# Attention followed by two gated MLPs on one core: layer 2's weights decoded from layer 1's last eight steps on, output copies issued before their sums, weight reloads and decode buffers moved

## The chip, the cores and the metric

The kernel runs on one core of one Trainium2 chip. The metric is the device time of one execution in microseconds (us), the median of several runs. The engines are PE (TensorE, the matrix engine), DVE (VectorE), ACT (ScalarE), POOL (GpSimd) and SP (SyncE, which here only issues DMAs). Each engine works through its own queue in order; semaphores tie the queues together.

## The reference

```
attention: q, k, v are (4, 12, 448, 64); rmsnorm of q and k with g_q, g_k; softmax(q k^T / 8) v
x  = attention output as 1792 tokens x 768
x  = ((x @ w_a) * (x @ w_b)) @ w_out                      # layer 1, d_ff = 1536
out = (sigmoid(x @ w_gate) * (x @ w_val)) @ w_out2        # layer 2, same sizes
```

All six weight matrices arrive as 64-bit floats; attention's inputs are 32-bit.

## The kernel before, in words

Attention comes first and is not touched. Each layer is then done as a seven-product block scheme (2 x 2 quadrants with sums and differences of quadrants, so that seven products take the place of eight). Every product is taken in three matmuls: each operand is split into a high part (`xh`, `wh`, `gh`, made by ACT's cast) and a rest (`xl`, `wl`, `gl`, made by a subtraction on DVE), and PE adds high*high, low*high and high*low.

**First part of a layer** (`first_part`): 84 events. An event is a pair (m, p): block m of 12 (even m: w_a or w_gate, odd m: w_b or w_val), product p of 7. It has 18 matmuls (two halves of the columns, three 128-row chunks, three matmuls each), line 872. The list `events` is the order by hand. Products 1 and 2 of one m share a PSUM bank: product 2 adds onto product 1, but only after ACT has copied product 1 out (line 924, `u<-mm`). Products 6, 7 and 4 share a bank in the same way; there ACT first puts a seed into it (`mm<-u`, line 846). Product 6's copy is line 928.

**Weights of the first part** (`weights`): quadrants of the 64-bit weights are loaded into `raw` (two buffers), then decoded to 32-bit in a tile `d` by one ACT operation (line 658) and three DVE operations (659, 661, 665). Event p may need a difference of quadrants (DVE, line 720), then ACT casts `wh` (line 724) and DVE makes `wl` (line 607, the helper's line). For m of 2 and 3 two quadrants are decoded early, stored to DRAM (`bd`, line 701) and loaded again when needed (line 716). Between the events the output weights are decoded too, always into tile `d8`, and stored to DRAM (`wd`). `prepare` advances decoding and splitting by small steps between the matmuls; `decodes` may run about three events ahead.

**Left operands** (`operands`): sums of the input's quadrants (DVE, line 788, called S1 to S4), each cast (`xh`, ACT, 779) and its rest (`xl`, DVE). In layer 1 the four quadrants are loaded from DRAM by `stage_in`.

**Second part** (`second_part`): 42 steps, seven products by six blocks f. In layer 1 a step has three units of six matmuls (line 1109), in layer 2 seven tiles of three (line 1119). `step(k)` prepares the operands of step k+3: DVE difference `d` (1005), in some products a difference `u` (1023), ACT casts `wh` (1008) and `gh` (1035), DVE rests. At the last f of a product each unit's PSUM is copied out by ACT (`ah<-mm`, lines 1138, 1142, 1146); after products 6 and 7 DVE adds a sum (line 1084, `more`), and `finish` makes layer 2's input of it: an ACT cast (line 610, `xh`) and a subtraction on POOL (`xl`). The next product adds onto the same banks, so PE waits for the copies. In layer 1's last three steps `prepare(1, ..., 8)` begins layer 2's weights.

Every engine's queue is written in program order (`manual_schedule`); nothing reorders it.

## Time and profile before

| | |
|---|---|
| median of 3 runs | 1340.98 us (1340.57 to 1344.35) |
| the profiled execution | 1341.52 us, its span 1339.4 us |
| PE busy | 1250.6 us (93%) |
| DVE busy | 1004.9 us (75%) |
| ACT busy | 704.2 us (53%) |
| POOL busy | 203.6 us (15%) |
| mean granted TensorE clock | 0.977 |

The span runs from the first to the last instruction. A busy share is an average over stages: attention fills the first 320 us or so, layer 1 lies between 317 and 842 us, layer 2 after that.

### The profile page before, as it was taken

The page shows a single profiled execution, that of the slowest core. Times are in us where ns is not written, and L with a number is a line of the kernel's source. Part 1 is how long each engine was busy: PE and PEld are TensorE (multiplying, and loading weights), DVE is VectorE, ACT ScalarE, POOL GpSimd, SP SyncE. Part 2 cuts the span into 40 slices and gives each one's busy share as a digit, 9 for nine tenths or more (in the row PEclk, how much of TensorE's full clock was granted, in tenths as well). Part 3 has the DMA queues.
Part 4 walks back from the last instruction along what each step waited for, and adds up shares of the span by engine and source line. Part 5 has one row for each costly group of instructions (what it writes and reads, how often), then busy time and mean ns, then how long its engine had stood idle before and what let it go on. Part 6 is the DMA issues. An engine that isn't in the chain of part 4 may idle for free.

```text
span 1339.4 us, 19161 instructions
## 1 busy us (share of the span) xinstructions
PE 1250.6 (93%) x6468; PEld 1114.6 (83%) x6468; DVE 1004.9 (75%) x1723; ACT 704.2 (53%) x1411; POOL 203.6 (15%) x272
## 2 busy tenths in 40 slices
PE   5999998898888999999999988789999999999997
PEld 4988887787767888887888877678888888899997
DVE  7999999987686778777558686786678777567583
ACT  3888888786353343443444644543354453444643
POOL 5565567740000000000002011000000000000000
PEclk9999999999889999999999988889999999999999
DMA  5677767665613456555486552413456555486674
GB/s 139 171 178 184 186 179 199 193 154 177 234 38 121 139 167 200 172 158 182 154 285 218 167 182 70 130 59 105 128 170 200 169 171 187 142 292 219 198 251 117
DMA packets 160433, 227.20 MB, mean 170 GB/s; under 512 B 26920, under 2 KB 134992, under 8 KB 160336
## 3 DMA queue, kind: packets, MB, share of 16 engines
q1 hardware_dynamic: 160336, 225.99, 55.5%
q8 instruction: 51, 0.84, 0.3%
q14 instruction: 46, 0.38, 0.1%
HBM read 147.46 MB, written 54.35 MB: 151 GB/s over the span
## 4 chain that ended last, share of the span: by engine, by line
PE 48%; DVE 22%; DMA 10%; ACT 10%; issue 4%; POOL 2%; SPq 2%; ACTq 0%; DVEq 0%; POOLq 0%
PE mm L872 23%; PE mm L1119 10%; PE mm L1109 7%; PE pv L407 3%; PE s L332 2%; DMA wd<-d 2%; DVE d L665 2%; DVE u L896 2%; DVE wl L607 2%; DVE raw L661 2%; DMA d<-bd 2%; DVE xl L607 2%; ACT wh L724 2%; DMA qk<-in_k_dram 1%; DVE d L720 1%
## 5 line engine op out<-in xcount | busy, mean ns | idle before, releaser
L872 PE MATMUL mm<-xh,wh 128*128 128x512 f32 (+1 forms) x1008 | 376.3, 373 | 37.5 <-ACT u L924 17.1
L872 PE MATMUL mm<-xl,wh 128*128 128x512 f32 (+1 forms) x1008 | 375.0, 372 | 5.9 <-DVE xl L607 5.9
L872 PE MATMUL mm<-xh,wl 128*128 128x512 f32 (+1 forms) x1008 | 375.4, 372 | 0.3 <-DVE wl L607 0.3
L607 DVE TENSOR_TENSOR wl<-d,wh 128x384 fp32r<-128x384 f32 x252 | 144.3, 573 | 153.4 <-ACT wh L724 91.9
L872 PEld LDWEIGHTS mm<-xh,wh 128*128 128x128 f32 x1008 | 193.5, 192 | 67.5 <-ACT u L924 18.6
L872 PEld LDWEIGHTS mm<-xl,wh 128*128 128x128 f32 x1008 | 193.7, 192 | 31.2 <-DVE xl L607 7.8
L872 PEld LDWEIGHTS mm<-xh,wl 128*128 128x128 f32 x1008 | 193.3, 192 | 22.7 <-DVE wl L607 0.8
L724 ACT CAST wh<-d 128x384 fp32r<-128x384 f32 x168 | 85.9, 512 | 205.4 <-DVE d L720 196.6
L658 ACT ACTIVATE d<-raw 128x384 f32<-128x384 f32 x144 | 80.4, 558 | 98.1 <-DMA wd<-d 41.1
L1008 ACT CAST wh<-d 128x384 fp32r<-128x384 f32 x84 | 43.2, 514 | 146.0 <-PE mm L1119 43.0
L344 ACT ACTIVATE P<-s,nm 128x448 f32<-128x448 f32 x168 | 107.9, 646 | 13.3 <-DVE nm L337 12.7
L395 DVE TENSOR_TENSOR pl<-tr,ph 128x512 fp32r<-128x512 f32 (+2 forms) x168 | 100.7, 611 | 9.4 <-ACT ph L391 7.9
L337 DVE TENSOR_REDUCE nm<-s 128x1 f32<-128x448 f32 x168 | 100.1, 616 | 5.1 <-PE s L332 5.1
L1109 PE MATMUL mm<-gh,wh 128*128 128x512 f32 x252 | 95.1, 377 | 8.5 <-ACT ah L1142 4.1
L1119 PE MATMUL mm<-wh,gh 128*128 128x384 f32 x294 | 98.8, 336 | 1.0 <-ACT ah L1142 0.8
L1119 PE MATMUL mm<-wl,gh 128*128 128x384 f32 x294 | 98.6, 335 | 0.0
L1119 PE MATMUL mm<-wh,gl 128*128 128x384 f32 x294 | 98.5, 335 | 0.0
L665 DVE SCALAR_TENSOR_TENSOR d<-d,raw 128x384 uint32<-128x384 uint32 x144 | 80.2, 557 | 23.4 <-ACT d L658 13.3
L391 ACT CAST ph<-tr 128x512 fp32r<-128x512 f32 (+2 forms) x168 | 85.6, 541 | 18.3 <-PE tr L377 12.6
L1109 PE MATMUL mm<-gl,wh 128*128 128x512 f32 x252 | 94.9, 377 | 0.0
L1109 PE MATMUL mm<-gh,wl 128*128 128x512 f32 x252 | 94.5, 375 | 0.0
L661 DVE SCALAR_TENSOR_TENSOR raw<-raw 128x384 uint32<-128x384 uint32 x144 | 80.4, 559 | 3.9
(161 smaller groups left out, 2293.5 us busy)
## 6 DMA issues: line engine op xcount, KB each, us to landing
gd<-u SPq DMA_DIRECT2D x60, 448.0 KB
u<-gd SPq DMA_DIRECT2D x60, 448.0 KB
d<-wd SPq DMA_DIRECT2D x132, 192.0 KB
raw<-in_moe_w_out_dram SPq DMA_DIRECT2D x48, 384.0 KB
wd<-d SPq DMA_DIRECT2D x72, 192.0 KB
KK<-KH SPq DMA_DIRECT2D x92, 112.0 KB
raw<-in_moe_w_a_dram SPq DMA_DIRECT2D x24, 384.0 KB
raw<-in_moe_w_b_dram SPq DMA_DIRECT2D x24, 384.0 KB
```

Source lines behind the costliest of these rows:

```text
L337: nc.vector.tensor_reduce(out=d["nm"][:, t:t + 1], in_=d["ps"][t], axis=AX.X, op=ALU.max, negate=True)
L344: nc.scalar.activation(out=e, in_=d["ps"].pop(t), func=AF.Exp, bias=d["nm"][:, t:t + 1], accum_out=d["sum"][:, t:t + 1])
L391: nc.scalar.copy(out=d["x", j, z][1], in_=tr)
L395: nc.vector.tensor_tensor(out=pl, in0=tr, in1=f32(ph), op=ALU.subtract)
L607: eng.tensor_tensor(out=lo, in0=t, in1=f32(hi), op=ALU.subtract)
L658: nc.scalar.activation(out=f32(t), in_=f32(high), func=AF.Copy, scale=2.0 ** -112)
L661: nc.vector.scalar_tensor_tensor(out=low, in0=high, scalar=0x80000000, in1=low, op0=ALU.bitwise_and, op1=ALU.bitwise_or)
L665: nc.vector.scalar_tensor_tensor(out=t, in0=t, scalar=3, in1=low, op0=ALU.logical_shift_left, op1=ALU.bitwise_or)
L724: nc.scalar.copy(out=hi, in_=t)
L872: nc.tensor.matmul(ps[:, o:o + size], w[:, P * c:P * c + P], x[:, o:o + size], start=(p in (1, 5) and c == 0 and z == 0), stop=(c == KC - ...
L1109: nc.tensor.matmul(ps[:, o:o + size], w[:, P * un:P * un + P], g[:, o:o + size], start=(p in (1, 5) and f == 0 and z == 0), stop=(f == HF ...
L1119: nc.tensor.matmul(ps[:, o:o + HB], g[:, P * t:P * t + P], w, start=(p in (1, 5) and f == 0 and z == 0), stop=(f == HF - 1 and z == 2), sk ...
```

## The change

1. **Layer 2's weights begin earlier.** In `second_part` of layer 1 one small step of `prepare(1, ...)` runs in every tick of the last eight steps (six ticks in a step), in place of eight steps at once after each of the last ones. The first eight of them only let the raw loads fly. The last six steps leave tiles d0, d2, d4 to layer 2, and its decoding waits for a tile until layer 1 has given it up.
2. **Order of the first three events in layer 2**: (0,1), (1,1), (0,2) in place of (0,1), (0,2), (1,1).
3. **Output copies of all units first, then the sums**: after products 6 and 7 of a second part, ACT's copies follow each other; the sums (`more`) and `finish` go to a list of which each tick takes one.
4. **Up to four raw loads at first**: among the first ten quadrants of a layer up to four are under way, two of them in `u` tiles.
5. **Reloads moved**: the quadrants of m = 2 and 3 stored in DRAM are loaded back as soon as their tile is free (after product 7, or one event after product 4, of m - 2). Product 4's difference of quadrants is taken at product 7.
6. **Decode tiles**: output weights alternate between d5 and d8; quadrant 1 of later blocks goes to d1.
7. **A12 of layer 1** is loaded from DRAM inside the operands' first loop instead of ahead of it.

No instruction is added or taken away; each engine has the same number of them.

```
-    events = [(0, 1), (0, 2), (1, 1), (2, 1), (1, 2), (3, 1), (2, 2), (3, 2)]
+    begun = [(2, 1), (1, 2), (3, 1), (2, 2), (3, 2)]
+    orders = [[(0, 1), (0, 2), (1, 1)] + begun + events, [(0, 1), (1, 1), (0, 2)] + begun + events]
...
+        def fill():
+            while wanted and len(loaded) < (4 if total - len(wanted) < 10 and len(free_u) >= 3 else 2):
+                load()
...
+            if [t for t, _ in loaded].count(None) >= 2:
+                tag, u = take_u()
+                r = u[:, 0:2 * HB].bitcast(U32).rearrange("p (f w) -> p f w", w=2)
+            else:
+                r = rawp.tile([P, HB, 2], U32, tag="raw", name="raw")
...
-            load()
-            load()
+            fill()
+            for _ in range(1 if l == 0 else 8):
+                yield
...
-                    t = dec("d8")
+                    k += 1
+                    t = dec("d5" if k % 2 else "d8")
...
+                        if q == 1 and m >= EARLY:
+                            tag = "d1"
+                        if l == 1:
+                            while held[0] is not None and tag not in held[0]:
+                                yield
...
-                if 2 <= m < EARLY and p in (5, 4):
-                    q = 0 if p == 5 else 2
-                    B[m, q] = dec(f"d{4 * (m % 2) + q}")
-                    nc.sync.dma_start(out=B[m, q], in_=bd[l][m % 2][q // 2])
+                if again:
+                    reload(*again.pop(0))
...
+                    if p == 7:
+                        nc.vector.tensor_tensor(out=B[m, 2], in0=B[m, 2], in1=B[m, 0], op=ALU.subtract)
+                        if m + 2 < EARLY:
+                            reload(m + 2, 0)
+                        yield True
+                if p == 4 and m + 2 < EARLY:
+                    again.append((m + 2, 2))
...
+        kept_d = ("d0", "d2", "d4") if l == 0 else ()
...
+        def tick(k):
+            step(k)
+            if after:
+                after.pop(0)()
+            if l == 0 and k >= NS - 8:
+                prepare(1, max(-1, AHEAD - NS + k), 1)
...
                         nc.scalar.copy(out=sums("a", un), in_=ps)
-                        more("c", un)
-                        finish(l, 0, 1, un, unit, sums("c", un))
+                        after.append(partial(more, "c", un))
+                        finals.append(partial(finish, l, 0, 1, un, unit, sums("c", un)))
...
+                after += finals
+                finals.clear()
...
-                if l == 0 and k > NS - 4:
-                    prepare(1, AHEAD - NS + k, 8)
```

ACT's queue where product 7 of layer 1's second part ends (`ah<-mm` are the copies of the three units, `xh<-al` the casts of `finish`, `wh` and `gh` step operands, `d<-raw` a decode). Before:

```order
L1142 COPY ah<-mm 128x896
L610 CAST xh<-al 128x896
L1142 COPY ah<-mm 128x896
L610 CAST xh<-al 128x896
L1142 COPY ah<-mm 128x896
L610 CAST xh<-al 128x896
L1008 CAST wh<-d 128x384
L1035 CAST gh<-u_9226 128x896
```

The same place now:

```order
L1201 COPY ah<-mm 128x896
L673 ACTIVATE d_9340<-raw 128x384
L1201 COPY ah<-mm 128x896 x2
L1058 CAST wh<-d 128x384
L1085 CAST gh<-u_9234 128x896
L673 ACTIVATE d_9370<-raw 128x384
L613 CAST xh<-al 128x896 x3
```

The casts that wait for DVE's sums have moved behind the copies, and a decode of layer 2 has come in between the first copy and the other two.

ACT's queue from the end of layer 1's second part into layer 2's first events (`u<-mm` of line 924 is the copy of a product 1). Before:

```order
L658 ACTIVATE d_9526<-raw 128x384
L1146 COPY ah<-mm 128x896 x3
L658 ACTIVATE d_9554<-raw 128x384
L724 CAST wh<-d_9489 128x384
L658 ACTIVATE d_9566<-raw 128x384
L924 COPY u_9594<-mm 128x896
L724 CAST wh<-d_9514 128x384
L779 CAST xh<-al 128x896
L931 ACT_TABLE_LOAD
L931 ACTIVATE u_9623<-mm 128x896
```

The same place now:

```order
L763 CAST wh<-d_9403 128x384
L1205 COPY ah<-mm 128x896 x3
L673 ACTIVATE d_9568<-u_9442 128x384
L763 CAST wh<-d_9431 128x384
L968 COPY u_9594<-mm 128x896
L763 CAST wh<-d_9477 128x384
L820 CAST xh<-al 128x896
L968 COPY u_9624<-mm 128x896
L763 CAST wh<-d_9507 128x384
L673 ACTIVATE d_9639<-raw 128x384
```

One decode stands between the output copies and the first `u<-mm` where two stood, and a second copy of a product 1 has come ahead of the gate's activation.

SP's queue in layer 1, where the stored quadrants are loaded back (`d<-bd`; `gd<-u` stores gated blocks). Before:

```order
L899 DMA gd_0_1_99<-u_5594 128x896
L647 DMA raw<-in_moe_w_b_dram 128x3x256 x2
L716 DMA d_5856<-bd_0_0_230 128x384
L649 DMA raw<-in_moe_w_out_dram 128x768
L899 DMA gd_1_0_104<-u_5710 128x896
L899 DMA gd_3_0_116<-u_5674 128x896
L716 DMA d_5947<-bd_1_0_232 128x384
```

The same place now:

```order
L943 DMA gd_0_1_99<-u_5594 128x896
L739 DMA d_5651<-bd_0_0_230 128x384
L662 DMA raw<-in_moe_w_b_dram 128x3x256
L739 DMA d_5800<-bd_1_0_232 128x384
L662 DMA raw<-in_moe_w_b_dram 128x3x256
L739 DMA d_5861<-bd_0_1_231 128x384
L664 DMA raw<-in_moe_w_out_dram 128x768
```

Three reloads now stand ahead of the first output-weight load, where one reload stood ahead of it.

## Rows read from the trace of the kernel before

**Rows 1.** The page: busy shares, granted clock by fortieths of the span (tenths).

```profile
PE 1250.6 (93%) x6468; PEld 1114.6 (83%) x6468; DVE 1004.9 (75%) x1723; ACT 704.2 (53%) x1411; POOL 203.6 (15%) x272
...
PEclk9999999999889999999999988889999999999999
```

**Rows 2.** Windows, a steady stretch: busy (instructions) per engine, clock, DMA share, GB/s.

```profile
480.00:560.00 80.00, 80.00 (x394) 71.19 (x393) 64.04 (x119) 34.69 (x60) 0.00 (x0) 1.00 0.57 173
```

**Rows 3.** Windows cut at event and step borders where PE lost time.

```profile
346.83:395.11 48.28, 35.96 (x128) 29.32 (x128) 39.49 (x54) 25.01 (x35) 0.00 (x0) 0.79 0.28 93
409.74:431.08 21.34, 16.97 (x74) 13.89 (x73) 16.12 (x25) 7.40 (x13) 0.00 (x0) 0.92 0.34 115
618.76:638.28 19.52, 16.73 (x73) 14.15 (x73) 12.86 (x25) 9.02 (x16) 0.00 (x0) 0.91 0.57 185
782.62:796.26 13.64, 10.20 (x37) 8.38 (x37) 10.02 (x8) 5.79 (x7) 6.58 (x3) 0.75 0.18 60
807.27:826.78 19.51, 15.44 (x56) 12.53 (x55) 13.41 (x12) 8.84 (x13) 6.27 (x3) 0.74 0.21 68
841.46:857.39 15.93, 9.12 (x37) 7.63 (x37) 10.24 (x18) 8.88 (x13) 0.00 (x0) 0.79 0.55 167
872.02:883.95 11.93, 9.14 (x37) 7.70 (x37) 11.35 (x15) 5.94 (x9) 0.00 (x0) 0.86 0.21 73
925.66:935.70 10.04, 7.60 (x38) 6.51 (x38) 6.25 (x12) 5.28 (x9) 0.00 (x0) 1.00 0.35 114
943.03:952.48 9.45, 7.56 (x37) 6.50 (x37) 6.58 (x12) 3.81 (x7) 0.00 (x0) 1.00 0.19 47
970.80:979.90 9.10, 7.60 (x37) 6.50 (x37) 7.22 (x11) 3.25 (x6) 0.00 (x0) 1.00 0.54 178
1126.80:1144.28 17.48, 15.19 (x73) 13.00 (x73) 11.30 (x22) 8.17 (x15) 0.00 (x0) 1.00 0.54 174
```

**Rows 4.** ACT's timeline at layer 2's start: start, us, instruction, idle before.

```profile
837.11 0.58 ACT L658 ACTIVATE d<-raw 128x384 f32<-128x384 f32 x1 [2.28 <-issue]
...
850.68 0.56 ACT L658 ACTIVATE d<-raw 128x384 f32<-128x384 f32 x1 [1.30 <-DMA raw<-in_moe_w_val_dram]
851.14 0.90 ACT L924 COPY u<-mm 128x896 f32<-128x896 f32 x1
```

**Rows 5.** SP's timeline, raw loads of layer 2.

```profile
807.12 0.96 SPq L647 DMA_DIRECT2D raw<-in_moe_w_gate_dram  x2
833.80 0.37 SPq L647 DMA_DIRECT2D raw<-in_moe_w_val_dram  x1
```

**Rows 6.** Waits at the start of layer 1 (300 to 440 us), DVE and ACT.

```profile
DVE d L720 <- DMA d<-bd: 8.6, 3, 3.9
DVE raw L659 <- DMA raw<-in_moe_w_a_dram: 6.2, 3, 5.5
...
ACT d L658 <- DMA raw<-in_moe_w_a_dram: 10.0, 1, 10.0
```

**Rows 7.** DVE's waits for reloads at the start of layer 2 (840 to 980 us).

```profile
DVE d L720 <- DMA d<-bd: 11.1, 4, 3.9
```

**Rows 8.** ACT's waits for the output weights' tile, 440 to 640 us.

```profile
ACT d L658 <- DMA wd<-d: 22.4, 13, 3.9
```

**Rows 9.** Groups by line: DVE's differences of quadrants, busy us and mean ns.

```profile
L720 DVE TENSOR_TENSOR d<-d,d 128x384 f32<-128x384 f32 x96 | 53.0, 552 | 22.5 <-DMA d<-bd 22.5
```

**Rows 10.** ACT's timeline where product 7 ends in layer 1.

```profile
811.16 0.90 ACT L1142 COPY ah<-mm 128x896 f32<-128x896 f32 x1
813.41 0.94 ACT L610 CAST xh<-al 128x896 fp32r<-128x896 f32 x1 [1.36 <-DVE al L1084]
814.26 0.90 ACT L1142 COPY ah<-mm 128x896 f32<-128x896 f32 x1
```

**Rows 11.** DVE's timeline in layer 1's product 7.

```profile
781.92 1.08 DVE L1084 TENSOR_TENSOR ah<-ah 128x896 f32<-128x896 f32 x1
784.81 2.29 DVE L1084 TENSOR_TENSOR ah<-ah 128x896 f32<-128x896 f32 x1 [1.81 <-ACT ah L1138]
...
798.53 1.09 DVE L607 TENSOR_TENSOR gl<-u,gh 128x896 fp32r<-128x896 f32 x1 [0.54 <-ACT gh L1035]
...
802.10 1.09 DVE L607 TENSOR_TENSOR gl<-u,gh 128x896 fp32r<-128x896 f32 x1 [0.54 <-ACT gh L1035]
```

**Rows 12.** POOL and DVE after product 2, where three splits follow each other.

```profile
715.05 7.05 POOL L607 TENSOR_TENSOR xl<-al,xh 128x896 fp32r<-128x896 f32 x3 [404.04 <-DMA wd<-d]
...
718.92 1.20 DVE L607 TENSOR_TENSOR wl<-d,wh 128x384 fp32r<-128x384 f32 x1 [3.29 <-ACT wh L1008]
720.05 3.01 DVE L607 TENSOR_TENSOR gl<-u,gh 128x896 fp32r<-128x896 f32 x1
```

More of the change, by code (lines that the diff above doesn't have):

```diff
@@ L1 @@
 from contextlib import ExitStack
+from functools import partial
 from itertools import chain
@@ L573, in attention_then_two_gated_mlps @@
     events.append((NF - 1, 4))
-    NE = len(events)
+    orders = [[(0, 1), (0, 2), (1, 1)] + begun + events, [(0, 1), (1, 1), (0, 2)] + begun + events]
+    NE = len(orders[0])
     NS = len(PASSES) * HF
@@ L630, in weights @@
         plan = []
+        events = orders[l]
         k = 0
@@ L641, in weights @@
         loaded = []
+        total = len(wanted)
+        def fill():
+            while wanted and len(loaded) < (4 if total - len(wanted) < 10 and len(free_u) >= 3 else 2):
+                load()
         def load():
             n, j, q = wanted.pop(0)
-            r = rawp.tile([P, HB, 2], U32, tag="raw", name="raw")
+            tag = None
+            if [t for t, _ in loaded].count(None) >= 2:
[3 more added lines that the diff above has]
+                r = rawp.tile([P, HB, 2], U32, tag="raw", name="raw")
             if n < 2:
@@ L649, in load @@
                 nc.sync.dma_start(out=r.rearrange("p f w -> p (f w)"), in_=quadrant(l, n, j, q))
-            loaded.append(r)
+            loaded.append((tag, r))
         def decode(t):
-            r = loaded.pop(0)
+            tag, r = loaded.pop(0)
             t = t.bitcast(U32)
@@ L667, in decode @@
             )
-            if wanted:
-                load()
+            if tag:
+                free_u.append(tag)
+            fill()
             yield
@@ L680, in decodes @@
         def decodes():
-            e = -1
-            load()
-            load()
+            e = k = -1
+            fill()
+            for _ in range(1 if l == 0 else 8):
+                yield
             for x, m, p in plan:
@@ L694, in decodes @@
                         spilled = 2 <= m < EARLY and p < 3
-                        t = dec(f"d{4 * (m % 2) + (q + 1 if spilled else q)}")
+                        tag = f"d{4 * (m % 2) + (q + 1 if spilled else q)}"
+                        if q == 1 and m >= EARLY:
[3 more added lines that the diff above has]
+                                yield
+                            if held[0] is not None:
+                                held[0].remove(tag)
+                        t = dec(tag)
                         B[m, q] = t
@@ L707, in decodes, with reload @@
             decoded[l] = NE
+        again = []
+        def reload(m, q):
+            B[m, q] = dec(f"d{4 * (m % 2) + q}")
+            nc.sync.dma_start(out=B[m, q], in_=bd[l][m % 2][q // 2])
         def splits():
@@ L764, in operands @@
         at = where[l]
-        a, b, c12, d = (staged[l][n] for n in ("A21", "A22", "A12", "A11"))
+        a, b, d = (staged[l][n] for n in ("A21", "A22", "A11"))
         casts, rests = [], []
@@ L795, in operands @@
             to("S1", c, t[c])
+            if l == 0:
+                stage_in(0, "A12", c)
             yield
@@ L812, in operands @@
             tt(t3, d[c], a[c], ALU.subtract)
-            tt(t4, c12[c], t[c], ALU.subtract)
+            tt(t4, staged[l]["A12"][c], t[c], ALU.subtract)
             to("S4", c, t4, tag4)
@@ L836, in first_part @@
         st, late, held = {}, [], {}
+        events = orders[l]
         more = None
@@ L988, in loads @@
                 gl[k] = tag, u
-                while len(free_d) < len(W_AT[p]):
+                mine = lambda: [t for t in free_d if k < NS - HF or t not in kept_d]
+                while len(mine()) < len(W_AT[p]):
                     yield
@@ L992, in loads @@
                 for q in W_AT[p]:
-                    tag = free_d.pop(0)
+                    tag = mine()[0]
+                    free_d.remove(tag)
                     t = decp.tile([P, HB], F32, tag=tag, name="d")
@@ L1113, in second_part @@
                                 )
-                            step(k)
+                            tick(k)
                     else:
@@ L1123, in second_part @@
                                 )
-                            step(k)
+                            tick(k)
                     if f < HF - 1:
@@ L1138, in second_part @@
                         nc.scalar.copy(out=sums("a", un), in_=ps)
-                        more("c", un)
-                        finish(l, 0, 1, un, unit, sums("c", un))
+                        after.append(partial(more, "c", un))
+                        finals.append(partial(finish, l, 0, 1, un, unit, sums("c", un)))
                     elif p == 7:
                         nc.scalar.copy(out=sums("a", un), in_=ps)
-                        more("b", un)
-                        finish(l, 1, 1, un, unit, sums("b", un))
+                        after.append(partial(more, "b", un))
+                        finals.append(partial(finish, l, 1, 1, un, unit, sums("b", un)))
                     else:
@@ L1151, in second_part @@
                         seed(len(seeds))
+                after += finals
+                finals.clear()
                 del GI[k], WI[k]
                 k += 1
-                if l == 0 and k > NS - 4:
-                    prepare(1, AHEAD - NS + k, 8)
                 yield
+        assert not after
+        held[0] = None
         if l == 0:
@@ L1199, in attention_then_two_gated_mlps @@
         begin_mm("mm1", 3)
-        for n in ("A22", "A12"):
-            for c in range(KC):
-                stage_in(0, n, c)
+        for c in range(KC):
+            stage_in(0, "A22", c)
         ready[0] = True
```

9 lines of the change are left out of this document (7 added, 2 removed).

## The prediction

> **What bounds the kernel now.** I read the page first: PE is busy 93% of the span, DVE 75%, ACT 53%, and the granted clock dips in two places only, slices 11 and 12 and slices 24 to 27 [rows 1]. Those are the beginning of layer 1 and the passage from layer 1 to layer 2. What can be won must therefore be PE's idle time and slow clock there, not work: the change adds and removes no instruction. Next I took PE's pace in a steady stretch: 394 matmuls in 80 us [rows 2], so an event or a step of 18 matmuls takes 3.66 us. Then I followed the list of events and steps along PE's instructions and cut windows exactly at their borders wherever one lasted longer than that [rows 3]; a row may count a matmul or two that hang over its edge, the program has 18 to an event. The loss of a window is its length less 3.66 us for each event:
>
> - events 5 to 11 of layer 1, (3,1) to (0,7): 48.3 for 7, loss 22.7
> - events 16 to 19 of layer 1: 21.3 for 4, loss 6.7
> - events 71 to 74 of layer 1: 19.5 for 4, loss 4.9
> - layer 1's second part, first two steps of product 7: 13.6 for 2, loss 6.3
> - its last step of product 7 and the first two of product 4: 19.5 for 3, loss 8.5
> - events 0 and 1 of layer 2: 15.9 for 2, loss 8.6
> - its events 6 and 7: 11.9 for 2, loss 4.6
> - its events 18 and 19, 22 and 23, 29 and 30: 2.7, 2.1 and 1.8
> - its events 71 to 74: 17.5 for 4, loss 2.9
>
> In the windows with the largest losses the clock stands at 0.74 to 0.79, so part of each loss is matmuls at the lower level (1.2 GHz) after PE had idled; it goes when the idling goes. The waits of ACT and DVE in the same stretches then say what PE waited for.
>
> **The change part by part.**
>
> *Layer 2's start.* ACT's decode at 850.68 had waited for its raw load, and the copy of product 1 at 851.14 came right behind it in ACT's queue [rows 4]; PE's event (0,2) cannot add onto that bank before. After the change the quadrants are loaded eight steps before the end, four at a time, and event (1,1) on another bank comes between (0,1) and (0,2), so the copy has 3.66 us. The load is not the risk: one issued at 833.80 [rows 5] had its decode running at 837.11 [rows 4], 3.3 us. Its window's loss goes: -8.6. Bounds: -4, half of it, if a decode still waits ahead of the copy, and -8.6, all there is. I take the whole, since two independent edits remove the same wait.
>
> *Reloads.* DVE waited 8.6 us in three waits for reloaded quadrants in layer 1's start [rows 6] and 11.1 us in four in layer 2's [rows 7]; behind each wait stood the gates' multiplications and ACT's seeds. They now are issued at least four events (14.6 us) before their use, and the longest wait was 3.9. The losses of events 16 to 19 in layer 1 and 18 to 30 in layer 2 sum to 13.3. I take -12, since the gates behind them are a chain of DVE and ACT of their own; bounds -6 (that chain holds half) and -13.3.
>
> *Output weights' tile.* Decoding into d8 had to wait until the tile was stored: 22.4 us in thirteen waits between 440 and 640 us, the longest 3.9 [rows 8]. Most lie under PE's work; where two output tiles follow each other, in events 71 to 74, they reach PE. With two tiles in turn a store has a whole decode more. The two windows lose 4.9 and 2.9: I take -7, bounds -3 (the raw load, still two deep there, is late next) and -7.8. Tile d1 now serves quadrant 1 of odd blocks too; its last reader is three events older, so I cost that at nothing, covered by those 11 us.
>
> *Four raw loads at the start of layer 1.* ACT waited 10.0 us in one piece for a raw load, DVE 5.5 [rows 6], while the input's quadrants were being loaded ahead of it. The ninth and tenth weight quadrants are now issued before those. But the loss of events 9 to 11 is DVE's: it makes the sums and rests of the operands one after the other, and PE takes them as they come. What PE gains is what DVE stands idle less, 5.5, less the two product-4 differences that now come earlier in DVE's queue at 0.55 each [rows 9]: -4.4. Bounds: 0 (another load is late instead) and -10.0. Moving A12's loads behind the others lies under the same DVE work and costs nothing; without that cover it would cost the three loads' time, which the upper bound holds.
>
> *Copies before sums.* Before, each unit's copy waited for the unit before it: copy 811.16, DVE's sum, cast 813.41, next copy 814.26 [rows 10]. Now the three copies follow each other, 0.90 each, and a unit of PE is 1.22, so after product 6 PE should not wait: -6.3. But the work only moves. DVE has three sums of 1.08 to do, and POOL's three splits then come back to back and hold DVE up: the second sum took 2.29 [rows 11], and in the 7.05 us of three splits after product 2 DVE got one operation done and a second begun [rows 12]. So DVE falls about 3 + 5 = 8 us behind. It cannot recover: in product 7 its step takes 802.10 - 798.53 = 3.57 [rows 11] against PE's 3.66. At the end of product 7 ACT's first copy stands behind the operands for three steps later, which wait for DVE, and is late by what DVE is: I let the second window keep its 8.5 and take -6.3 + 0.3 = -6. Bounds: 0 (both windows keep theirs, in other places) and -14.8 (both go).
>
> The Trainium skill speaks against this part ("SBUF — State Buffer", Who interferes with whom): a DVE operation with two SBUF inputs and a POOL operation that reads SBUF exclude each other for a whole instruction. The rows agree with it for a subtraction. By the rule the two-input operations of layer 2's decoding, which now stand among product 4's splits, are shut out as well, and the sum would be that of rival 1; by the rows alone, which show no such operation beside POOL, it is the one below.
>
> *Not changed:* events 6 to 11 of layer 2. DVE's order of sums there is the old one and begins at the same distance behind PE: 0, between -4.6 and +4. Layer 2's second part: 0, within 1.
>
> **The sum.** 8.6 + 12 + 7 + 4.4 + 6 = 38.0. The profiled execution took 1341.5 (span 1339.4 and 2.1 around it), so 1303.5; the median shown is 0.5 lower: 1303. By the favourable bounds the gain is 8.6 + 13.3 + 7.8 + 10 + 14.8 + 4.6 = 59, by the others 4 + 6 + 3 + 0 + 0 - 4 = 9.
>
> **Rivals.**
> 1. *DVE is the next bound and gives back what the moves win.* The windows with DVE nearly always busy (11.35 of 11.93 us in events 6 and 7 of layer 2 [rows 3]) speak for it. Then layer 1's passage gains 0, layer 2's start 4 (its decodes end late), layer 1's start 0: 38 - 6 - 4.6 - 4.4 = 23, 1318. Against it: DVE is busy only 13.4 of 19.5 us in the last window of layer 1.
> 2. *The waits go with all that hung on them.* Both windows of layer 1's second part vanish (14.8 for 6), the raw term is 10 for 4.4: 38 + 8.8 + 5.6 = 52, 1288. For it: with a fast clock kept, PE's own units free banks sooner. Against it: DVE's pace.
> 3. *Slower: layer 2's decodes stop layer 1.* A decode stands in ACT's queue between the copies that PE waits for, and its loads stand in SP's queue among layer 1's. If each of the eight first decodes waited as long as DVE's longest, 5.5 us [rows 6], 44 us would be lost, 38 - 44 = -6: 1347. It decides from 4.75 us for each. Against it: raw loads issued at 807.12 [rows 5] lay there long before their use.
> 4. *It doesn't do what it says:* the early loads wait for `u` tiles and the rest cancels, 1341.
>
> **How the numbers follow.** Forecast 0.53, rival 1 0.22, rival 2 0.16, rival 3 0.05, rival 4 0.04. A measurement here can tell about 0.3%, 4 us. Forecast and rivals 1 and 2 are faster by more: 0.91; rival 4 is the same, 0.04; rival 3 slower, 0.05. The forecast's own range is 1294 to 1313. With rivals 1 and 2 nearly whole the range is 1284 to 1325; outside lie rivals 3 and 4 and the tails.
>
> **What would show it.** PE runs through events 0 to 2 of layer 2 without a gap; no DVE wait on the reloads above 1 us; no ACT wait on the store of output weights that PE follows; the first steps of product 7 at 3.66 us, but a wait of PE for ACT's copy of some 4 to 5 us as product 4 begins; events 9 and 11 of layer 1 and 7 and 11 of layer 2 still late. The forecast is wrong if PE waits for a copy behind a decode in layer 1's last eight steps, or if product 4 begins without a wait.

## The result and the profile after

The changed kernel takes 1299.2 us in the median of four runs (1298.56 to 1302.48), beside 1341.4 us of the kernel before, now a median of four runs as well: a ratio of 0.9687, 95% interval 0.9664 to 0.9709, or 42 us less. The forecast was 1303 with a range of 1284 to 1325. The profiled execution is the longest of the four, 1302.48 us with a span of 1300.6.

The page of the changed kernel (busy shares; granted clock by fortieths of the span):

```profile
PE 1237.5 (95%) x6468; PEld 1106.8 (85%) x6468; DVE 1005.5 (77%) x1723; ACT 702.7 (54%) x1411; POOL 207.2 (16%) x272
...
PEclk9999999999989999999999999989999999999999
```

The instruction counts are those of [rows 1]: no work has gone. PE is busy 13 us less with the same matmuls, and the clock dips in two slices where it dipped in six: fewer of them ran at the lower level. Windows of the changed kernel at the same events and steps as [rows 3], in the same columns. Events 22, 23, 29 and 30 of layer 2, which lose nothing now, are left out. The sixth row is new, the last two steps of layer 1; it ends 0.16 us inside layer 2's first event:

```profile
350.36:393.43 43.07, 32.48 (x127) 26.39 (x127) 39.61 (x55) 23.66 (x33) 0.00 (x0) 0.84 0.29 93
408.07:422.73 14.66, 14.66 (x74) 13.09 (x73) 11.04 (x19) 5.54 (x9) 0.00 (x0) 1.00 0.44 156
609.62:624.28 14.66, 14.66 (x74) 13.07 (x73) 12.35 (x24) 7.47 (x13) 0.00 (x0) 1.00 0.57 174
768.34:775.68 7.34, 7.34 (x37) 6.54 (x37) 7.33 (x10) 5.82 (x8) 2.60 (x1) 1.00 0.26 75
786.69:803.89 17.20, 12.82 (x55) 11.10 (x55) 14.49 (x20) 11.57 (x17) 2.12 (x1) 0.90 0.75 253
811.23:820.59 9.36, 8.11 (x38) 6.71 (x38) 8.23 (x16) 6.02 (x11) 0.00 (x0) 1.00 0.06 9
820.43:827.75 7.32, 7.32 (x37) 6.51 (x37) 6.65 (x12) 3.92 (x6) 0.00 (x0) 1.00 0.57 182
842.37:854.29 11.92, 9.14 (x38) 7.83 (x37) 11.34 (x15) 5.93 (x9) 0.00 (x0) 0.86 0.21 73
896.99:904.33 7.34, 7.34 (x38) 6.55 (x37) 4.87 (x8) 3.13 (x5) 0.00 (x0) 1.00 0.38 138
1091.23:1105.90 14.67, 14.67 (x73) 13.10 (x73) 12.37 (x24) 7.58 (x13) 0.00 (x0) 1.00 0.56 178
```

Where length and PE's busy time are the same number, PE ran without a gap: events 16 to 19 and 71 to 74 of layer 1, the first two steps of product 7, and events 0 and 1, 18 and 19, 71 to 74 of layer 2. Four of the rows still lose time: events 5 to 11 of layer 1, the border from product 7 to product 4, the last two steps of layer 1, and events 6 and 7 of layer 2, which are as they were (11.92 for 11.93). In no row are layer 1's first three events, right behind attention: they lose 10.5 us, and lost 11.3 before.

DVE's longest wait at the start of layer 2 (840 to 980 us):

```profile
DVE wl L610 <- ACT wh L763: 20.7, 23, 2.9
```

The other six come to 3.6 us or less each, and none of them is for a reload; the 11.1 us of [rows 7] are gone.

The loss by place, worked out as in the prediction (time between the starts of two events or steps less 3.66 us for each), of both kernels and of every experiment. "L1a" is layer 1's first part, "L1b" its second, "L2a" layer 2's first; the numbers are events or steps.

| kernel | L1a 5-12 | L1a 16-19 | L1a 71-74 | L1b 30-31 | L1b 35-37 | L1b 40-41 | all of L1b | L2a 0-1 | L2a 6-11 | L2a 18-30 | L2a 71-74 |
|---|---|---|---|---|---|---|---|---|---|---|---|
| before | 22.6 | 6.7 | 4.9 | 6.3 | 8.5 | 0.0 | 16.5 | 8.6 | 9.7 | 6.6 | 2.8 |
| changed | 17.4 | 0.0 | 0.0 | 0.0 | 6.2 | 1.9 | 9.4 | 0.0 | 10.7 | 0.0 | 0.0 |
| u_copies | 17.1 | 0.0 | 0.0 | 6.6 | 8.5 | 0.0 | 16.5 | 0.0 | 9.6 | 0.0 | 0.0 |
| u_reload | 18.1 | 6.9 | 0.0 | 0.0 | 7.3 | 0.8 | 9.4 | 0.0 | 9.7 | 7.4 | 0.0 |
| u_tile | 16.4 | 0.0 | 1.7 | 0.0 | 6.2 | 1.9 | 9.5 | 0.0 | 8.1 | 0.0 | 1.8 |
| u_reltile | 16.7 | 6.9 | 4.3 | 0.0 | 6.0 | 1.9 | 9.5 | 0.0 | 9.7 | 9.6 | 4.7 |
| u_raws | 18.8 | 0.0 | 0.0 | 0.0 | 6.7 | 1.4 | 9.4 | 0.1 | 11.2 | 0.0 | 0.0 |
| u_a12 | 18.0 | 0.0 | 0.0 | 0.0 | 7.0 | 1.1 | 9.5 | 0.0 | 9.4 | 0.0 | 0.0 |
| u_raws_a12 | 23.1 | 0.0 | 0.0 | 0.0 | 7.3 | 0.8 | 9.4 | 0.2 | 9.6 | 0.0 | 0.0 |
| u_early | 17.5 | 0.0 | 0.0 | 0.0 | 7.1 | 0.0 | 8.5 | 0.0 | 10.5 | 0.0 | 0.0 |
| u_order | 16.1 | 0.0 | 0.0 | 0.0 | 7.2 | 0.9 | 9.5 | 1.2 | 10.7 | 0.0 | 0.0 |
| n_p6dve | 17.3 | 0.0 | 0.0 | 0.0 | 4.1 | 1.9 | 7.3 | 0.0 | 10.7 | 0.0 | 0.0 |
| n_alldve | 17.2 | 0.0 | 0.0 | 0.0 | 4.1 | 0.0 | 5.0 | 0.0 | 9.7 | 0.0 | 0.0 |
| n_first_pace | 17.5 | 0.0 | 0.0 | 0.0 | 3.6 | 3.8 | 10.1 | 0.0 | 10.3 | 0.0 | 0.0 |

From before to changed the columns (without that of all of L1b) fall by 5.2 + 6.7 + 4.9 + 6.3 + 2.3 - 1.9 + 8.6 - 1.0 + 6.6 + 2.8 = 40.5 us. The span fell by 1339.4 - 1300.6 = 38.8; layer 1's first event began at 321.5 us in this execution and at 317.2 in that of before, and among the experiments, whose attention is the same code, it begins between 316.4 and 321.6. So some 5 us of difference between two executions come from ahead of the changed part, and the place table is the finer measure: where a kernel's edit doesn't reach, most columns repeat within 0.1. The columns L1a 5-12 and L2a 6-11 don't: where the edit lies elsewhere they still run from 16.1 to 17.5 and from 8.1 to 10.7. The columns L1b 35-37 and 40-41 trade up to 1.1 us with each other (6.2 and 1.9, 7.3 and 0.8), so it is their sum that repeats, 7.9 to 8.1.

### The profile page after: what moved, and what is told of

Same layout as the page of the kernel before. It is cut to its first block, busy times and chain, and to the rows that moved or that the text cites. A ratio compares the mean times of both kernels' runs of the same rounds, so it can differ in the third digit from the quotient of the medians.

```text
span 1300.6 us, 19144 instructions
## 1 busy us (share of the span) xinstructions
PE 1237.5 (95%) x6468; PEld 1106.8 (85%) x6468; DVE 1005.5 (77%) x1723; ACT 702.7 (54%) x1411; POOL 207.2 (16%) x272
## 4 chain that ended last, share of the span: by engine, by line
PE 59%; DVE 7%; ACT 3%; issue 2%; DMA 1%; SPq 0%; ACTq 0%; DVEq 0%
PE mm L916 42%; PE mm L1178 9%; PE mm L1168 8%; DVE xl L610 2%; ACT gh L1085 1%; DVE wl L610 1%; DVE gl L610 1%; DVE u L1073 1%; DVE d L680 1%; DVE d L1055 0%; DMA u<-gd 0%; DVE u L829 0%; DVE d L751 0%; DVE al L829 0%; DMA d<-wd 0%
## 5 line engine op out<-in xcount | busy, mean ns | idle before, releaser
L916 PE MATMUL mm<-xh,wh 128*128 128x512 f32 (+1 forms) x1008 | 371.6, 369 | 15.5 <-ACT u L968 6.2
L345 ACT ACTIVATE P<-s,nm 128x448 f32<-128x448 f32 x168 | 107.8, 645 | 16.4 <-DVE nm L338 15.9
L673 ACT ACTIVATE d<-raw 128x384 f32<-128x384 f32 x136 | 75.8, 557 | 68.1 <-DMA raw<-in_moe_w_gate_dram 14.2
L680 DVE SCALAR_TENSOR_TENSOR d<-d,raw 128x384 uint32<-128x384 uint32 x136 | 77.4, 569 | 12.3 <-ACT d L673 2.4
L610 DVE TENSOR_TENSOR gl<-u,gh 128x896 fp32r<-128x896 f32 x60 | 69.3, 1156 | 18.7 <-ACT gh L1085 18.6
```

Of the source, the lines that this page charges most:

```text
L345: nc.scalar.activation(out=e, in_=d["ps"].pop(t), func=AF.Exp, bias=d["nm"][:, t:t + 1], accum_out=d["sum"][:, t:t + 1])
L610: eng.tensor_tensor(out=lo, in0=t, in1=f32(hi), op=ALU.subtract)
L673: nc.scalar.activation(out=f32(t), in_=f32(high), func=AF.Copy, scale=2.0 ** -112)
L680: nc.vector.scalar_tensor_tensor(out=t, in0=t, scalar=3, in1=low, op0=ALU.logical_shift_left, op1=ALU.bitwise_or)
L916: nc.tensor.matmul(ps[:, o:o + size], w[:, P * c:P * c + P], x[:, o:o + size], start=(p in (1, 5) and c == 0 and z == 0), stop=(c == KC - ...
```

## The experiments

The first nine undo parts of the change, the other three change what it left. Each time is a median of four or five runs, with the ratio to the kernel before timed beside it; the changed kernel's own ratio is 0.9687, and the half width of an interval is 2 to 4 us, so that effects under 4 us are read from the table.

### u_copies: copies and sums in the old order

```diff
-                        after.append(partial(more, "c", un))
-                        finals.append(partial(finish, l, 0, 1, un, unit, sums("c", un)))
+                        more("c", un)
+                        finish(l, 0, 1, un, unit, sums("c", un))
```

and the same for product 7.

> The changed kernel with one part undone: after products 6 and 7 each unit's copy, sum, cast and split follow each other again, as before. If the copies' part is worth what the place table of the two traces says (second part of layer 1: loss 16.4 before, 9.4 after), the time rises by 7 us to about 1306, product 7's first two steps lose about 6 us again and the passage to product 4 about 8.5. Rival, the second window was won by something else (early decodes, a fast clock): it loses 6 as in the changed kernel, and the rise is 6.3 - 2 or about 4 us. Rival, DVE gives back all: no rise.

1304.39 us, 0.9733 (0.9706 to 0.976). The second part of layer 1 loses 16.5 us again, in each of its columns within 0.3 of what it lost before, 7.0 more than in the changed kernel. The part is worth 7, as the first theory has it.

### u_reload: quadrants loaded back when needed

```diff
-                if again:
-                    reload(*again.pop(0))
+                if 2 <= m < EARLY and p in (5, 4):
+                    reload(m, 0 if p == 5 else 2)
...
-                    if p != 4:
-                        nc.vector.tensor_tensor(out=B[m, t], in0=a, in1=b, op=ALU.subtract)
-                    yield True
-                    if p == 7:
+                    nc.vector.tensor_tensor(out=B[m, t], in0=a, in1=b, op=ALU.subtract)
+                    yield True
```

(the rest of the block under `p == 7` goes too, and the list `again`).

> The changed kernel with one part undone: stored quadrants are loaded back when the product that needs them comes (products 5 and 4), and product 4's difference is made there. Theory: events 16 to 19 of layer 1 lose 6 to 7 us again and events 18 to 30 of layer 2 about 6.6, so the time rises by 13 us to about 1312, and DVE shows three and four waits for reloads. Rival, half of that loss was the gates' own chain or another load in SP's queue: a rise of 6 us or less. Rival, the place only moves: no rise in the total, losses in events 16 to 30 paid for by smaller ones in events 6 to 11.

1314.21 us, 0.9798 (0.9773 to 0.9822). Events 16 to 19 lose 6.9 us and the three pairs of layer 2 lose 7.4, 14.3 together; in the table's other columns nothing is given back. DVE's waits for reloads are back as well (840 to 980 us, beside 11.1 in [rows 7]):

```profile
DVE d L750 <- DMA d<-bd: 11.8, 4, 4.2
```

The gates' own chain held none of that loss. The edit also puts product 4's difference back in its old place, and the two aren't told apart here.

### u_tile: output weights always in d8

```diff
-                    t = dec("d5" if k % 2 else "d8")
+                    t = dec("d8")
...
-                        if q == 1 and m >= EARLY:
-                            tag = "d1"
```

> The changed kernel with one part undone: output weights are always decoded into tile d8, and quadrant 1 of later odd blocks into d5 as before. Theory: ACT waits again for the store of the tile and events 71 to 74 lose 4.9 and 2.9 us, so the time rises by 7 to 8 us to about 1307. Rival, the loss there came from the raw load that is two deep, or from the seeds: a rise under 3 us.

1301.24 us, 0.9707 (0.9682 to 0.9731). Windows of events 71 to 74, in layer 1 and in layer 2, in the columns of the windows above:

```profile
605.66:621.98 16.32, 14.93 (x74) 13.02 (x74) 11.13 (x22) 6.85 (x13) 0.00 (x0) 1.00 0.50 163
1086.40:1102.84 16.44, 14.93 (x74) 13.05 (x74) 11.09 (x22) 6.96 (x14) 0.00 (x0) 1.00 0.48 164
```

ACT's wait for the store in this kernel, 425 to 628 us:

```profile
ACT d L673 <- DMA wd<-d: 17.4, 12, 4.0
```

The wait is back nearly as before [rows 8], but PE loses only 1.7 and 1.8 of the 4.9 and 2.8 us. The tile alone is worth 3.5, half of what I had given it.

### u_reltile: both of these undone

The edits of u_reload and u_tile together.

> The changed kernel with two parts undone, the reloads and the output weights' tile. Undone alone the reloads cost 14.3 us in the place table, the tile 3.4. If the two parts work on different losses, events 71 to 74 lose 1.6 and 1.7 us and the time is about 1317. If the moved difference of product 4 had won part of the tile's loss (it stands in DVE's queue and in the chain to the seed), those events lose 4.9 and 2.9 again as before, and the time is about 1321.

1323.82 us, 0.9855 (0.983 to 0.9881). The windows of events 71 to 74 again:

```profile
617.49:636.45 18.96, 16.71 (x73) 14.36 (x73) 12.59 (x24) 8.90 (x15) 0.00 (x0) 0.91 0.57 186
1112.01:1131.36 19.35, 16.74 (x73) 14.37 (x73) 12.61 (x24) 8.97 (x16) 0.00 (x0) 0.91 0.54 183
```

No quadrant is loaded back at those blocks, so of the first edit only the difference of product 4 can act there. With it back in its old place too, these events lose 4.3 and 4.7 us, and the clock falls to 0.91 in both. Before, it did so in layer 1 only; in layer 2 it stood at 1.00 [rows 3], and there the 4.7 us are more than the 2.8 of before. The columns of the two parts sum to 25.5, where each undone alone cost 14.3 and 3.5: the two parts cover for each other in events 71 to 74 and in 29 and 30. ACT's waits for the store are about the same in both kernels (4.8 us in u_tile's first window, 4.5 here), so what they cost PE depends on how late the difference of product 4 already is.

### u_raws: two raw loads at most

```diff
-            while wanted and len(loaded) < (4 if total - len(wanted) < 10 and len(free_u) >= 3 else 2):
+            while wanted and len(loaded) < (2 if total - len(wanted) < 10 and len(free_u) >= 3 else 2):
```

> The changed kernel with one part undone: never more than two raw loads under way, in either layer. Theory: the start of layer 1 loses what the four loads won, about 5 us in events 5 to 11, and layer 2's start stays without a gap because its loads begin eight steps early: about 1304. Rival, the four loads are also what clears layer 2's start: another 4 to 8 us in its events 0 and 1, about 1311. Rival, the input's loads were the wait, so that A12's move won it: no rise.

1303.02 us, 0.972 (0.9696 to 0.9744). Events 5 to 12 lose 18.8 us, 1.3 to 2.7 more than the kernels whose edits lie elsewhere; layer 2's start loses 0.1. So four loads are not what clears layer 2's start, and they aren't by themselves what won 5 us in layer 1.

### u_a12: A12 loaded ahead of the operands' loop

```diff
-            if l == 0:
-                stage_in(0, "A12", c)
...
-        for c in range(KC):
-            stage_in(0, "A22", c)
+        for n in ("A22", "A12"):
+            for c in range(KC):
+                stage_in(0, n, c)
```

> The changed kernel with one part undone: A12 of layer 1 is loaded from DRAM ahead of the operands' loop again, so its three loads stand ahead of weight loads in SP's queue. The prediction cost that part at nothing: 1299, events 5 to 11 of layer 1 lose 17.4 as in the changed kernel. Rival, seen from the run with two raw loads, where they lost 18.8 of the 22.6 of before: this part won the rest, so they lose about 21 to 22 and the time is about 1303.

1300.52 us, 0.9685 (0.9662 to 0.9708). Events 5 to 12 lose 18.0 us. That is neither 17.4 nor 21, and hardly outside the spread of that column: inconclusive by itself.

### u_raws_a12: both of these undone

> The changed kernel with two parts undone, the four raw loads and A12's place among the loads. Undone alone, events 5 to 12 of layer 1 lost 18.8 and 18.1 us, against 16.1 to 17.6 in the kernels that keep both, and 22.7 in the kernel before. If either part hides the same late load, both together cost more than their sum: 22 to 23 us, and the time is about 1305. If they are independent: about 20, 1302. If the difference to before came from the order of layer 1's other loads: 18 to 19, 1301.

1304.02 us, 0.9733 (0.9713 to 0.9753). Events 5 to 11, and PE's longest wait in them:

```profile
347.17:395.06 47.89, 34.26 (x128) 27.98 (x128) 40.09 (x55) 25.00 (x35) 0.00 (x0) 0.81 0.27 91
```

```profile
PE mm L914 <- ACT u L966: 6.4, 2, 4.5
```

The window is as long as before (47.89 for 48.28), the column 23.1 for 22.6. (Not all kernels that keep both parts lose 16.1 to 17.6 us there: u_reload, whose edit moves other work into these events, loses 18.1, so 18.8 and 18.0 alone say little.) In events 5 to 8 by themselves the loss is 10.8 before, 3.9 to 5.6 in the kernels that keep both parts, 6.9 in u_raws, 6.1 in u_a12 and 10.1 here: either part alone keeps most of the 5 us, and both must be undone to lose it. ACT's longest wait for a weight load at the start of layer 1 shows the same, first here, then in u_raws:

```profile
ACT d L673 <- DMA raw<-in_moe_w_a_dram: 9.7, 1, 9.7
ACT d L673 <- DMA raw<-in_moe_w_a_dram: 6.4, 1, 6.4
```

It was 10.0 before [rows 6], and neither u_a12 nor the changed kernel has it. In SP's queue that load stands behind all six loads of A22 and A12 here and ahead of the last three in u_raws; with four loads under way (u_a12) it goes out ahead of all six. So whether two more weight loads go out early or three loads of A12 go out late, the weight quadrant gets ahead of A12.

### u_early: layer 2's weights begun in layer 1's last three steps

```diff
-            if l == 0 and k >= NS - 8:
-                prepare(1, max(-1, AHEAD - NS + k), 1)
...
+                if l == 0 and k > NS - 4:
+                    prepare(1, AHEAD - NS + k, 8)
```

and no tile is kept for layer 2; the eight empty steps ahead of layer 2's first decode go too.

> The changed kernel with one part undone: layer 2's weights are begun in layer 1's last three steps, eight small steps at once after each, as before; the new event order and the four loads stay. Theory of the prediction, two independent edits remove the same wait: layer 2's events 0 and 1 stay without a loss and the time stays at 1299, within 2; layer 1's last two steps win back their 2 us, since no decode stands among the output splits. Rival, the early loads do all of it: events 0 to 2 lose 8 to 9 us again, about 1306.

1300.99 us, 0.9688 (0.9665 to 0.9712). Layer 2's first two events lose nothing, and layer 1's second part loses 8.5 in place of 9.4. Its last two steps win back their 1.9 us, but the border before them loses 7.1 for 6.2, so 1.0 is won and not 2.

### u_order: the old order of layer 2's first events

```diff
-[(0, 1), (1, 1), (0, 2)] + begun + events]
+[(0, 1), (0, 2), (1, 1)] + begun + events]
```

> The changed kernel with one part undone: layer 2's first events are (0,1), (0,2), (1,1) as in layer 1. Theory of the prediction, two independent edits: no loss comes back, 1299 within 2. Rival, the order does part of it: even with the weights ready, event (0,2) waits for ACT's copy of (0,1) on the same bank, which is a copy of 0.90 and its way there, so 1 to 3 us come back, about 1301.

1300.82 us, 0.9688 (0.9664 to 0.9713). ACT's copy of event (0,1), and PE's waits around it (816 to 830 us):

```profile
820.48 0.91 ACT L968 COPY u<-mm 128x896 f32<-128x896 f32 x1 [1.89 <-PE mm L916]
```

```profile
PE mm L916 <- ACT u L968: 1.0, 1, 1.0
```

1.2 us of the 8.6 come back: ACT now stands idle until event (0,1) ends, and event (0,2) waits 1.0 for the copy itself; no decode is ahead of it. So either edit is nearly enough, the order for all 8.6 and the early weights for 7.4, as long as the rest of the change stands. Both undone together was not run, so it isn't shown that these two edits alone remove the wait.

### n_p6dve: product 6's rests on DVE

```diff
-                split(src, hi, lo, nc.gpsimd)
+                split(src, hi, lo, nc.vector if n == "A12" else nc.gpsimd)
```

The reason is in the changed kernel's own trace. PE's waits from 780 to 822 us (the first as product 4 begins, the second in layer 1's last two steps), and ACT's timeline ahead of that copy:

```profile
PE mm L1168 <- ACT ah L1201: 4.4, 1, 4.4
PE mm L1168 <- DVE gl L610: 1.2, 2, 0.6
```

```profile
792.68 0.51 ACT L1058 CAST wh<-d 128x384 fp32r<-128x384 f32 x1 [1.70 <-DVE d L1055]
793.10 0.93 ACT L1085 CAST gh<-u 128x896 fp32r<-128x896 f32 x1
793.94 0.90 ACT L1201 COPY ah<-mm 128x896 f32<-128x896 f32 x1
```

The copy comes last in a row of casts in which each `wh` waits for DVE's difference (1.70 us here). DVE had fallen behind eighteen microseconds earlier, beside POOL's three splits:

```profile
775.13 2.40 DVE L610 TENSOR_TENSOR wl<-d,wh 128x384 fp32r<-128x384 f32 x1
777.46 3.01 DVE L610 TENSOR_TENSOR gl<-u,gh 128x896 fp32r<-128x896 f32 x1
780.40 2.48 DVE L1055 TENSOR_TENSOR d<-d 128x384 f32<-128x384 f32 x1
782.80 1.08 DVE L1073 TENSOR_TENSOR u<-fl,u 128x896 f32<-128x896 f32 x1
783.80 0.55 DVE L610 TENSOR_TENSOR wl<-d,wh 128x384 fp32r<-128x384 f32 x1
```

```profile
773.08 9.38 POOL L610 TENSOR_TENSOR xl<-ah,xh 128x896 fp32r<-128x896 f32 x3 [64.97 <-ACT xh L613]
```

The first row's operation takes 0.55 when POOL is idle (last row of DVE's); beside POOL it takes 2.40.

> The changed kernel with product 6's three rests (layer 2's left operand A12) subtracted on DVE in place of POOL. In the changed kernel DVE had three operations beside these three POOL splits that took 2.4 to 3.0 us each, 5.7 us more than alone; on DVE the three rests are 3 x 1.09 = 3.3 us. Theory, DVE's lag behind POOL is what makes product 4 wait for its copy: the lag is 2.4 us smaller, the wait goes from 4.4 to about 2 and layer 1's second part loses 9.4 - 2.4 or about 7, time -2. Rival, the wait comes from DVE's amount of work in product 7 and not from POOL: DVE has 3.3 us more, the wait grows to 6 or 7, time +2 to +3. Rival, the wait is that of the queue order on ACT alone: no change.

1296.3 us, 0.9659 (0.9642 to 0.9677). DVE's three rests, and PE's wait for the copy (780 to 820 us):

```profile
769.91 3.08 DVE L610 TENSOR_TENSOR xl<-ah,xh 128x896 fp32r<-128x896 f32 x3
```

```profile
PE mm L1168 <- ACT ah L1201: 2.2, 1, 2.2
```

DVE has three operations more and is less late: 4.4 becomes 2.2, the second part of layer 1 loses 7.3 for 9.4. That is the number of the lock theory, and the two rivals give another sign or none. The times alone don't separate this kernel from the changed one (their intervals overlap); the table does. What holds the other 2.2 us was not taken apart.

### n_first_pace: copies ahead of the casts, and slower operand sums in layer 2

```diff
-            step(k)
-            if after:
+            hold = l == 0 and k == NS - HF - 1
+            if not hold:
+                step(k)
+            if after and not hold:
                 after.pop(0)()
...
-                        if ticks % 4 == 0:
+                        if ticks % (4 if l == 0 else 5) == 0:
```

> The changed kernel with two edits that lie far apart. First, in the last step of layer 1's product 7 no operand of a later step is prepared, so ACT's copies stand ahead of those casts: by the theory that the copy waits behind casts that wait for DVE, the 6.2 us at the border to product 4 fall to under 1.5; DVE then owes one step's operands, so one of the next steps may lose 1 to 3. By the rival that DVE's pace is the bound, the whole loss comes back in product 4's steps and layer 1's second part stays at 9.4. Second, in layer 2 the operand sums are advanced at every fifth tick in place of every fourth. If DVE's amount of work bounds events 6 to 11 of layer 2, their loss stays at 9.5 to 10.8 us in all, only its place moves; if it is the order (a product's copy behind casts that wait for early sums), it falls by 4.

1301.55 us, 0.9711 (0.9689 to 0.9733). PE's waits, 780 to 820 us:

```profile
PE mm L1170 <- ACT ah L1203: 3.0, 2, 1.6
PE mm L1170 <- DVE gl L610: 1.9, 1, 1.9
PE mm L1170 <- ACT gh L1085: 1.2, 1, 1.2
```

ACT in the last step of product 7, and the windows of steps 35 to 37 and 38 to 41:

```profile
787.22 0.90 ACT L1203 COPY ah<-mm 128x896 f32<-128x896 f32 x1
789.90 0.57 ACT L673 ACTIVATE d<-raw 128x384 f32<-128x384 f32 x1 [1.79 <-DMA raw<-in_moe_w_gate_dram]
790.37 1.70 ACT L1203 COPY ah<-mm 128x896 f32<-128x896 f32 x2
```

```profile
783.02:797.55 14.53, 11.56 (x55) 9.70 (x55) 11.28 (x17) 8.15 (x13) 0.00 (x0) 1.00 0.90 298
797.55:817.54 19.99, 16.95 (x74) 14.51 (x74) 18.80 (x27) 11.11 (x18) 7.61 (x3) 0.91 0.24 78
```

The first copy is early now, and a decode that waits for its raw load stands ahead of the other two: in place of one wait of 4.4 PE has two of 3.0 together. Three steps on, the operands are late: the border loses 3.6 for 6.2, product 4's last four steps 19.99 - 14.64 = 5.3 (5.2 without the end of the window, which lies in layer 2) with DVE busy 18.80 of 19.99 us, and layer 1's second part 10.1 for 9.4. In layer 2 the loss moves from events 6, 7 and 10 to event 11 and stays 10.3 in all. In both places what PE wins by going earlier is paid back where DVE is late.

That doesn't show that DVE's own work is too much in layer 1. Three of its operations in the second window stand beside POOL's splits here too, one of them an operand of product 4's steps:

```profile
799.92 2.37 DVE L676 SCALAR_TENSOR_TENSOR u<-u 128x384 uint32<-128x384 uint32 x1
802.22 2.48 DVE L1055 TENSOR_TENSOR d<-d 128x384 f32<-128x384 f32 x1
804.62 2.45 DVE L680 SCALAR_TENSOR_TENSOR d<-d,u 128x384 uint32<-128x384 uint32 x1
```

Alone they take 0.55 each, so 5.6 of the 18.80 us are POOL's doing. The earlier copies together with all rests on DVE were not run.

### n_alldve: all nine rests on DVE

```diff
-                split(src, hi, lo, nc.gpsimd)
+                split(src, hi, lo, nc.vector)
```

In the changed kernel, POOL's splits of product 7 and DVE beside them (the last two rows are behind the last split):

```profile
801.77 7.01 POOL L610 TENSOR_TENSOR xl<-al,xh 128x896 fp32r<-128x896 f32 x3 [19.31 <-DVE gl L610]
802.28 2.31 DVE L680 SCALAR_TENSOR_TENSOR d<-d,raw 128x384 uint32<-128x384 uint32 x1
804.51 2.28 DVE L674 TENSOR_SCALAR u<-u 128x384 uint32<-128x384 uint32 x1
806.82 2.37 DVE L676 SCALAR_TENSOR_TENSOR u<-u 128x384 uint32<-128x384 uint32 x1
809.12 0.55 DVE L1055 TENSOR_TENSOR d<-d 128x384 f32<-128x384 f32 x1
809.59 0.54 DVE L680 SCALAR_TENSOR_TENSOR d<-d,u 128x384 uint32<-128x384 uint32 x1
```

> The changed kernel with all nine rests of layer 2's left operands (made after products 2, 6 and 7 of layer 1's second part) subtracted on DVE; POOL does none. After product 6 that alone took 2.2 us off. After product 7 three decode operations stood beside three POOL splits and took 2.3 to 2.4 us each, 5.5 us more than alone, against 3 x 1.09 on DVE; the last two steps of product 4 lost 2.0 us. Theory, the lock between DVE and POOL is what those steps lose: they lose nothing, layer 1's second part goes from 7.2 to about 5, the time from 1296.3 to about 1294. Rival, product 4's end is bound by how much DVE has to do there (decodes, sums, operands): they lose 2 to 4 still, 1296 to 1298.

1295.52 us, 0.9652 (0.9635 to 0.9669). The last two steps of layer 1:

```profile
808.07:815.57 7.50, 7.50 (x38) 6.70 (x38) 6.47 (x14) 5.76 (x10) 0.00 (x0) 1.00 0.21 67
```

The last two steps run without a gap (the row ends 0.16 us late, as above), and layer 1's second part loses 5.0: of the 2.3 us less than in n_p6dve 1.9 are won in those steps, the rest where product 5 ends. This is the best version here: 0.9652 for 0.9687, with intervals that overlap a little, and 4.4 us less in the place it was made for. Against n_p6dve the times don't separate (0.9652 and 0.9659), the table does (5.0 and 7.3).

## Why the prediction was right, and where it wasn't

**Layer 2's start, -8.6.** Measured 8.6 in the place table. That either of two edits is enough is shown by u_early and u_order: with one gone at most 1.2 us return. That no other part of the change has a share in it is not shown, since both undone together was not run. So the earlier start of layer 2's weights wins nothing that the order of two events hasn't won, and layer 1's second part loses 1.0 more with its decodes in between (9.4 for 8.5).

**Reloads, -12.** Measured 13.3, and 14.3 when undone: the favourable bound. I had kept 1.3 for the gates' chain, and it held nothing. Part of the 13.3 may be product 4's moved difference, which u_reload undoes with the reloads.

**Output weights' tile, -7.** The windows did win 7.7 us, but this step gave them to the wrong part: the tile alone holds 3.5, the tile and the moved difference of product 4 together 9.0 (u_reltile, 1.3 more than the windows lost before). I had read the waits of ACT for the store, which reach PE only where DVE is late as well. The lower bound's reason, the raw load that is late next, didn't occur: with the tile in turn no window of events 71 to 74 loses anything.

**Four raw loads, -4.4.** Measured 5.2, and again the part named isn't the only owner. I had cost the move of A12's loads at nothing; it and the four loads each suffice for most of it (18.8 and 18.0 us lost without one), and without both the loss is 23.1. The place is the one forecast: all of the 5.2 was won in events 5 to 8, and events 9 to 11, which were said to be DVE's, lose 11.8 us in both kernels. That DVE is what they wait for fits its 39.61 busy us of 43.07 in the changed kernel's window; no run takes that work away.

**Copies before sums, -6.** Measured 7.0 (16.5 to 9.4), and in the form forecast: the first window goes, the second moves. The expected wait of 4 to 5 us for the copy as product 4 begins is 4.38, in one piece. The second window keeps 6.2 of the 8.5 that I let it keep whole, and 1.9 appear in the last two steps, which I had not named; that the two come to 8.1 is in part luck, since those 1.9 are neither there with the old order of copies (u_copies) nor without the early decodes (u_early). DVE's lag has the two sources named: three sums, 3.3 us, and operations stretched by POOL, (2.40 - 0.55) + (3.01 - 1.09) + (2.48 - 0.55) = 5.7; that POOL's part is a cause and not only beside it is shown by n_p6dve, for 2.2 of the 4.4 us. "It cannot recover" was too strong: the 3.57 of [rows 11] is the step of a product with two differences. The last three operand steps ahead of the late copy are product 4's, and they take 3.05 or 3.06 in the changed kernel:

```profile
791.01 1.09 DVE L610 TENSOR_TENSOR gl<-u,gh 128x896 fp32r<-128x896 f32 x1 [0.28 <-ACT gh L1085]
794.06 1.09 DVE L610 TENSOR_TENSOR gl<-u,gh 128x896 fp32r<-128x896 f32 x1 [0.28 <-ACT gh L1085]
```

So DVE wins back 0.6 us in each of them (3.66 - 3.05), which isn't enough in three steps.

The rule that was weighed there (the Trainium skill, "SBUF — State Buffer", Who interferes with whom) says that DVE operations with two SBUF inputs are shut out beside a POOL operation that reads SBUF; those of the decoding are such operations. The trace agrees: 2.31 and 2.37 us beside POOL, and 0.54 (last row shown under n_alldve) and 0.56 (the median of line 676) without it. Rival 1's time, 1318, doesn't follow all the same, since the lock's price there was 1.9 us, what n_alldve wins back in the last two steps; before those, PE ran through product 4 while DVE was shut out.

**Not changed.** Events 6 to 11 of layer 2 lose 10.7 for 9.7, within the bounds given and within that column's spread. n_first_pace speaks for DVE's work and against its order as the limit, with one other pace tried.

**The sum.** Forecast -38.0, measured -42.2 in the medians. By the terms 8.6 for 8.6, 13.3 for 12, 7.7 for 7, 5.2 for 4.4 and 7.0 for 6 make 41.8, less the 1.0 of layer 2's events 6 to 11: 40.8. Places that I had left out fell too (layer 1's first three events 0.8, its events 20 to 70 0.8, layer 2's events 31 to 70 0.3). These sums come from one profiled execution of each kernel and the 42.2 from medians with an interval of some 3 us either way, so the last 1 or 2 us are not resolved. The four terms that were taken under their whole windows each came out larger, by 0.7 to 1.3. Of the rivals, 2 didn't come (the second window stays), 3 didn't as priced (layer 2's decodes cost layer 1 the 1.0 us that u_early gives back; n_first_pace shows the mechanism once, a decode waiting 1.79 us for its load ahead of two copies), and 4 didn't. Of the signs named, PE's wait for the copy came as described, and events 9 and 11 of layer 1 and 7 and 11 of layer 2 are late still.

## What to carry to other kernels

A table of loss by place (the stretch less the same work at its steady pace) gave the worth of this rearrangement to within 5 us of 42, but it says what goes and not which edit takes it away: where several edits touch one queue, undo them singly and in pairs. A copy that frees a bank is as late as the latest thing ahead of it in its engine's queue, and moving it further forward (n_first_pace) won nothing here while the engine behind that wait was late itself. Three POOL subtractions that looked like free help cost DVE more time (5.7 us) than doing them itself (3.08).

## What the hardware showed beyond that

A DVE operation with one SBUF operand is shut out by POOL too: the shift of line 674 (`TENSOR_SCALAR`, 128 x 384 words, in place) took 2.28 us beside a split. Its group in the changed kernel, and that of line 676 (duration in ns, least, median, greatest):

```profile
L674 DVE TENSOR_SCALAR u<-u x8: 350/354/2279, 324.2 to 822.1; 128x384 uint32<-128x384 uint32 x8
L676 DVE SCALAR_TENSOR_TENSOR u<-u x8: 546/556/2369, 324.9 to 822.5; 128x384 uint32<-128x384 uint32 x8
```

The Trainium skill ("SBUF — State Buffer", Who interferes with whom) says that `tensor_scalar` can enter a mode that takes both of DVE's ports and then contends with POOL; the greatest of the row, 2279 for a median of 354, agrees. It is a single instance.
